# Value rows on ScalarE's queue, and the first rounding steps one stage later

## The chip, the cores and the metric

The kernel runs on one core of one Trainium2 chip. The metric is the device time of one execution in microseconds (us), lower is better. Where engines are named: TensorE (PE; PEld is its weight load), VectorE (DVE), ScalarE (ACT), GpSimd (POOL) and SyncE (SP, which only issues transfers).

## The reference

A retention layer (attention with a decay in place of the softmax) is followed by a feed-forward layer with the activation `h * erf(softplus(h))`. There are 8 batches, 8 heads, 576 tokens and 64 columns a head.

```python
scores = scale * np.matmul(q, k.transpose(0, 1, 3, 2))
Dmat = np.where(rel >= 0, gamma[:, None, None] ** rel[None, :, :], 0.0)
ret = scores * Dmat[None, :, :, :]
attn_out = np.matmul(ret, v)
# ... (B,H,S,D) -> (B*S, H*D) = x of 4608 x 512
h = x @ w_in                                  # w_in 512 x 2048
sp = np.maximum(h, 0.0) + np.log1p(np.exp(-np.abs(h)))
g = h * erf(sp)
out = g @ w_out                               # w_out 2048 x 512
```

## The kernel before

Attention is cut into 36 pieces of 128 tokens, counted from 0. Of each nine pieces the last is split: 64 tokens of each of two batches. Four pieces make a chunk of 512 tokens. A piece goes through three stages on TensorE: transposes of q and k, scores (masked by VectorE), and outputs, with a running state of k and v between the pieces of a batch.

```python
pieces = []
for b in range(0, B, 2):
    pieces += [[(b + j, s0, P, 0)] for j in range(2) for s0 in range(0, S - D, P)]
    pieces.append([(b + j, S - D, D, j * D) for j in range(2)])
...
SQUARES = 2 * PC        # from piece 8 on q comes in squares
SQUARES_K = 3 * PC      # from piece 12 on k comes in squares too
```

The "squares" are blocks laid out so that VectorE can transpose q and k in 32 x 32 blocks; earlier pieces are transposed by TensorE. Values `v` always come in rows, 256 bytes a packet, two transfers for a whole piece and four for a split one, into one of four buffers. Nearly all transfers are issued by SyncE, in the order in which they are written here:

```python
def load_squares(i, name, src):
    ...
            nc.sync.dma_start(out=t[...], in_=tokens[...])      # 4 for a piece, 8 for a split one

def load_rows(i, name, src, bufs):
    ...
    for b, s0, n, r0 in pieces[i]:
        for e in range(2):
            heads = src[b, e * NP : (e + 1) * NP, s0 : s0 + n, :]
            queue = nc.scalar if (name, i) == ("k", 0) else nc.sync
            queue.dma_start(out=t[r0 : r0 + n, e::2, :], in_=heads.rearrange("h p d -> p h d"))

def transposes(i):
    ...                                # q and k of the piece: kT, qT
    load(i + 2, "q")                   # squares of q, and of k from piece 12 on

def outputs(i):
    ...                                # o <- sT, v; o <- v, k; o <- qT, state; sums; x = scaled(1), scaled(0)
    load(i + 3, "kv")                  # rows of k and of v
    if i + 1 >= SQUARES:
        weigh_values(i + 1)            # GpSimd scales the rows of v by the decays

stages = [(transposes, 0), (scores, 0)]
for i in range(len(pieces)):
    stages += [(transposes, i + 1), (outputs, i), (scores, i + 1)]
```

Engines run their instructions in order. The buffers' semaphores and waits are set by the framework when the program is built.

The weights are rounded by VectorE, ScalarE and GpSimd before they are used. One part of the weights takes five steps, and between two steps the kernel may do other work:

```python
def rounding():
    while True:
        ...
        nc.scalar.activation(a_f, high_f, AF.Abs)
        nc.scalar.mul(out=r_f, in_=low, mul=2.0**-52)
        yield
        nc.vector.tensor_scalar(out=a_f, in0=a_f, ..., op0=ALU.max, op1=ALU.min)
        yield
        nc.vector.tensor_scalar(out=a, in0=a, ..., op0=ALU.logical_shift_left, op1=ALU.bitwise_and)
        yield
        nc.vector.scalar_tensor_tensor(out=a, in0=high, ..., op0=ALU.bitwise_and, op1=ALU.bitwise_or)
        yield
        ...                            # the rest: and, multiply, add
```

The order of the first stretch is written out in a string. `a` does the next attention stage, `l` loads rows of piece 2, `k` keeps TensorE warm with idle matmuls, `w` loads a part of the weights, a digit does so many rounding steps, `p` does a part of the first feed-forward product (`L565` in the profile), `s` stores x:

```python
for what in "alkakakawkakakawwaa3awa2aaa5ppppaa5wwppa5ppawappwcppa5ppaaapp5s":
    if what == "a":
        attend(done[0] + 1)
    ...
    else:
        round_weights(int(what))
```

Afterwards the attention stages are spread between the products of the feed-forward layer (`First`, `L511`, and `Second`, `L619`), each of which is evicted from PSUM by a copy of ScalarE or an addition of VectorE.

Of the kernel before, what the change touches and what calls it, by code (L numbers as in the profile page):

```python
# [54 lines left out]
def kernel(  # L55
# [10 lines left out]
    nc = tc.nc  # L66
# [53 lines left out]
    SQUARES_K = 3 * PC  # L120
# [15 lines left out]
    def load_rows(i, name, src, bufs):  # L136
        if name == "q":
            t = raw.tile([P, NP, P * D // SQ], FP32, tag="qs", name="raw_q", bufs=bufs)
            t = t.rearrange("p a x -> p (a x)")[:, : H * D].rearrange("p (h d) -> p h d", h=H)
        else:  # L140
            t = raw.tile([P, H, D], FP32, tag=name, name=f"raw_{name}", bufs=bufs)
        for b, s0, n, r0 in pieces[i]:
            for e in range(2):
                heads = src[b, e * NP : (e + 1) * NP, s0 : s0 + n, :]

                queue = nc.scalar if (name, i) == ("k", 0) else nc.sync
                queue.dma_start(out=t[r0 : r0 + n, e::2, :], in_=heads.rearrange("h p d -> p h d"))  # L147
        return t

    def load(i, names="qkv"):  # L150
        if i < len(pieces):
            t = loaded.setdefault(i, {})
            for name in names:
                src = {"q": q, "k": k, "v": v}[name]
                if name == "q" and i < SQUARES:
                    t["q"] = load_rows(i, "q", q, 2)
                elif name == "q":
                    t["qs"] = load_squares(i, "q", q)
                    if i >= SQUARES_K:
                        t["ks"] = load_squares(i, "k", k)  # L160
                elif name == "v" or i < SQUARES_K or len(pieces[i]) == 1:
                    t[name] = load_rows(i, name, src, 4)
# [69 lines left out]
    def load_weights():  # L232
        part = next(coming, None)
        if part is not None:
            t = wraw.tile([P, 2 * WP], UINT32, tag="wraw", name="wraw")
            for rows, src in part[0]:
                nc.sync.dma_start(out=t[rows].rearrange("p (h f) -> p h f", h=2), in_=src)
            words.append((t, *part[1:]))
# [49 lines left out]
    def round_weights(n=1):  # L288
        for _ in range(n):
            next(round_step, None)  # L290
# [174 lines left out]
    def attend(upto):  # L465
        while done[0] < min(upto, len(stages)):
            of, i = stages[done[0]]
            of(i)
            done[0] += 1
# [9 lines left out]
    def store_x(c):  # L479
        nc.sync.dma_start(out=xd[c], in_=x[0, c][:, :n_dc])  # L480
# [269 lines left out]
    def keep_busy(n):  # L750
        for _ in range(n):
            nc.tensor.matmul(idle[:, :P], lhsT=ones, rhs=ones, start=True, stop=True)
# [13 lines left out]

    for what in "alkakakawkakakawwaa3awa2aaa5ppppaa5wwppa5ppawappwcppa5ppaaapp5s":
        if what == "a":  # L770
            attend(done[0] + 1)
        elif what == "p":
            next(products)
        elif what == "s":
            store_x(0)
        elif what == "l":
            load(2, "kv")
        elif what == "c":
            nc.sync.dma_start(out=cst[:, CONST_FIRST:], in_=consts[:, CONST_FIRST:])
        elif what == "w":  # L780
            load_weights()
        elif what == "k":
            keep_busy(2)
        else:
            round_weights(int(what))
# [93 lines left out]
```

## Time and profile before

| what | value |
|---|---|
| time, median of 3 | 1020.92 us (1018.78 to 1022.29) |
| span of the profiled execution | 1019.8 us |
| TensorE clock granted | 1.000 |
| busy: TensorE / VectorE / ScalarE / GpSimd | 1008.4 / 662.0 / 390.0 / 120.0 us |
| moved by the transfers | 165.76 MB, mean 163 GB/s |
| packets under 512 bytes | 97376 of 146986 |

Busy time of an engine is the sum of its instructions; a matmul's end is modelled, so a full TensorE is not TensorE at its peak. The profile gives for each instruction what its engine waited for before it (the releaser). The attention pieces are loaded and computed in the first 318 us, with the feed-forward products of the first of four groups of weights running between them; after that only feed-forward work is left. A transfer shows as an issue on a queue (`SPq`, `ACTq`) and as a landing some microseconds later.

### The profile page before, as it was taken

To read this page: it belongs to the slowest core of one execution; us is meant where nothing else is said; L and a number is where in the kernel's file an instruction comes from. 1 tells how busy PE (TensorE), PEld (TensorE's weight loads), DVE (VectorE), ACT (ScalarE), POOL (GpSimd) and SP (SyncE) were. 2 spreads that over 40 slices of the span, in tenths; PEclk is the share of its full clock that TensorE was granted. 3 is DMA by queue.
4 is the path that set the end of the run, shared out by engine and by line. 5 is a ranking of instruction groups with operands and counts; after the bars stand their busy time and mean duration, and the time that the engine had idled before them with its cause. 6 is when DMAs were issued, how large, how long until landed. Compare 5 with 4: busy or idle time off the path is not lost.

```text
span 1019.8 us, 15964 instructions
## 1 busy us (share of the span) xinstructions
PE 1008.4 (99%) x6348; PEld 878.4 (86%) x6348; DVE 662.0 (65%) x1062; ACT 390.0 (38%) x481; POOL 120.0 (12%) x122
## 2 busy tenths in 40 slices
PE   8999999999999999999999999999999999999998
PEld 7788888887888888888888888888888888888887
DVE  3769867876976655666666666666667555555555
ACT  2354143233234443433343344434433333333332
POOL 2133121221212100010011001000100000000000
PEclk9999999999999999999999999999999999999999
DMA  9997989979976344544444344434333334444434
GB/s 195 205 245 171 237 193 220 241 159 248 245 160 240 115 158 147 162 159 146 166 146 145 130 165 159 145 145 145 145 124 124 135 124 131 125 131 139 124 88 119
DMA packets 146986, 165.76 MB, mean 163 GB/s; under 512 B 97376, under 2 KB 121568, under 8 KB 138848
## 3 DMA queue, kind: packets, MB, share of 16 engines
q1 hardware_dynamic: 144832, 163.57, 56.9%
q10 hardware_dynamic: 2080, 1.18, 0.5%
q8 instruction: 50, 0.82, 0.4%
q14 instruction: 24, 0.20, 0.1%
HBM read 117.52 MB, written 47.19 MB: 162 GB/s over the span
## 4 chain that ended last, share of the span: by engine, by line
PE 87%; DMA 6%; SPq 4%; DVE 2%; issue 0%; POOL 0%; ACT 0%; DVEq 0%; POOLq 0%; ACTq 0%
PE a L619 23%; PE a L511 22%; PE g L619 11%; PE g L511 11%; PE e L511 6%; PE e L619 6%; PE s L347 2%; PE o L365 2%; SPq L147 2%; SPq L131 2%; DMA raw_qs<-in_q_dram 1%; DMA raw_v<-in_v_dram 1%; DMA raw_ks<-in_k_dram 1%; DMA wraw<-in_moe_w_in_dram 1%; PE o L388 1%; PE o L377 1%
## 5 line engine op out<-in xcount | busy, mean ns | idle before, releaser
L511 PE MATMUL a<-x,wa 128*128 128x256 f32 x1088 | 257.3, 379 | 0.0
L511 PEld LDWEIGHTS a<-x,wa 128*128 128x128 f32 x1088 | 206.6, 190 | 28.2 <-issue 0.2
L619 PE MATMUL a<-wb,s 128*128 128x256 f32 x840 | 198.7, 380 | 0.0
L619 PEld LDWEIGHTS a<-wb,s 128*128 128x128 f32 x840 | 159.5, 190 | 22.0 <-ACT o L633 0.5
L99 DVE TENSOR_TENSOR t<-g,t 128x512 f32<-128x512 f32 x68 | 47.0, 690 | 148.3 <-ACT t L541 111.3
L511 PE MATMUL g<-x,wa 128*128 128x256 f32 x544 | 129.0, 380 | 0.0
L511 PEld LDWEIGHTS g<-x,wa 128*128 128x128 f32 x544 | 103.0, 190 | 14.3
L99 DVE TENSOR_TENSOR o<-a,o 128x512 f32<-128x512 f32 x104 | 71.5, 687 | 46.4 <-PE a L619 46.4
L536 ACT COPY t<-a 128x512 f32<-128x512 f32 x34 | 19.9, 585 | 177.7 <-PE a L511 177.7
L99 DVE TENSOR_TENSOR t<-t,s 128x1024 f32<-128x1024 f32 x72 | 85.0, 1222 | 0.0
L274 POOL TENSOR_TENSOR wraw<-wraw 128x512 f32<-128x512 f32 x28 | 29.4, 1051 | 446.0 <-DVE wraw L272 197.4
L580 ACT ACTIVATE s<-t 128x1024 f32<-128x1024 f32 x72 | 72.1, 1049 | 23.0 <-DVE t L99 23.0
L547 ACT COPY t<-a 128x512 f32<-128x512 f32 x34 | 19.9, 586 | 152.9 <-PE a L511 152.9
L99 DVE TENSOR_TENSOR x<-x 128x512 f32<-128x512 f32 x115 | 75.8, 693 | 1.2
L584 ACT ACTIVATE s<-s 128x1024 f32<-128x1024 f32 x72 | 72.1, 1048 | 0.4
L619 PE MATMUL g<-wb,s 128*128 128x256 f32 x280 | 66.8, 381 | 0.0
L619 PE MATMUL e<-wb,t 128*128 128x256 f32 x280 | 66.7, 381 | 0.0
L619 PE MATMUL g<-wb,t 128*128 128x256 f32 x280 | 66.2, 380 | 0.0
L619 PE MATMUL a<-wb,t 128*128 128x256 f32 x280 | 66.1, 379 | 0.0
L511 PE MATMUL e<-x,wa 128*128 128x256 f32 x272 | 64.9, 381 | 0.0
L541 ACT COPY t<-a 128x512 f32<-128x512 f32 x34 | 19.9, 585 | 108.7 <-PE a L511 108.7
L619 PEld LDWEIGHTS a<-wb,t 128*128 128x128 f32 x280 | 53.2, 190 | 7.2
(86 smaller groups left out, 1260.9 us busy)
## 6 DMA issues: line engine op xcount, KB each, us to landing
od<-o SPq DMA_DIRECT2D x54, 512.0 KB, 3.3
x<-xd SPq DMA_DIRECT2D x27, 1024.0 KB, 4.8
o<-od SPq DMA_DIRECT2D x27, 1024.0 KB, 5.0
raw_qs<-in_q_dram SPq DMA_DIRECT2D x96, 112.0 KB, 4.6
raw_ks<-in_k_dram SPq DMA_DIRECT2D x84, 112.0 KB, 4.1
xd<-x SPq DMA_DIRECT2D x9, 1024.0 KB, 5.5
raw_v<-in_v_dram SPq DMA_DIRECT2D x64, 128.0 KB, 4.4
wraw<-in_moe_w_in_dram SPq DMA_DIRECT2D x32, 256.0 KB, 5.8
```

Of the source, the lines that this page charges most:

```text
L99: nc.vector.tensor_tensor(out=out, in0=in0, in1=in1, op=op)
L131: nc.sync.dma_start(out=t[part * SQ : (part + 1) * SQ, :, at : at + m - SQ], in_=tokens[:, :, d0 : d0 + m - SQ])
L147: queue.dma_start(out=t[r0 : r0 + n, e::2, :], in_=heads.rearrange("h p d -> p h d"))
L274: engine.tensor_tensor(out=r_f, in0=high_f, in1=r_f, op=ALU.mult)
L347: nc.tensor.matmul(ps[e][:, p, :], lhsT=t["kT"][heads[e], p, :], rhs=t["qT"][heads[e], p, :], start=True, stop=True)
L365: nc.tensor.matmul(o[p % 2][heads[(e + p) % 2], p // 2, :], lhsT=t["v"][:, 2 * p + e, :], rhs=t["sT"][:, e, p, :], start=(p < 2), stop=(no ...
L511: nc.tensor.matmul(acc[:, j * TH : (j + 1) * TH], lhsT=weights["wa", self.g][:, a, d, j * P : (j + 1) * P], rhs=x[self.g, self.c][a][:, d, :],
L536: nc.scalar.copy(out=self.t1[:, 1], in_=self.a)
L541: nc.scalar.copy(out=self.t2[:, 1], in_=self.a)
L580: nc.scalar.activation(self.s[:, j], t, AF.Softplus)
L584: nc.scalar.activation(self.s[:, j], self.s[:, j], AF.Erf)
L619: nc.tensor.matmul(acc[:, tp, :], lhsT=left[:, j * TH + tp * P : j * TH + (tp + 1) * P], rhs=weights["wb", self.g][:, b, j, :], start=(sta ...
```

## The change

```diff
-                queue = nc.scalar if (name, i) == ("k", 0) else nc.sync
+
+                by_act = (name, i) == ("k", 0) or (name == "v" and i >= SQUARES_K)
+                queue = nc.scalar if by_act else nc.sync
                 queue.dma_start(out=t[r0 : r0 + n, e::2, :], in_=heads.rearrange("h p d -> p h d"))
...
-    for what in "alkakakawkakakawwaa3awa2aaa5ppppaa5wwppa5ppawappwcppa5ppaaapp5s":
+    for what in "alkakakawkakakawwaaa3wa2aaa5ppppaa5wwppa5ppawappwcppa5ppaaapp5s":
```

The first edit moves the rows of values of piece 12 and all later ones (the 13th piece on) from SyncE's queue to ScalarE's. SyncE has then fewer transfers to issue, and the squares of q and k stand behind fewer others in its queue; the values are issued where ScalarE stands in its own instructions. Nothing is added to what is moved.

The second edit exchanges one `3` and one `a` of the string: the first three steps of the first part's rounding (`3`) now come behind the outputs of the third piece (`a`) and not ahead of them, so that VectorE does the sums and the scaling of those outputs first. Both edits leave all arithmetic as it is.

## The prediction

> **What bounds the kernel now.** I read the page first: engine totals, then who waited for whom on TensorE, then busy time by stretches of 10 us.
>
> ```profile
> span 1019.8 us, 15964 instructions
> PE 1008.4 (99%) x6348; PEld 878.4 (86%) x6348; DVE 662.0 (65%) x1062; ACT 390.0 (38%) x481; POOL 120.0 (12%) x122
> PE s L347 <- DVE kT L326: 2.4, 1, 2.4
> PE pt_q L332 <- DVE x L99: 1.5, 1, 1.5
> PE pt_k L332 <- DMA raw_k<-in_k_dram: 1.0, 2, 0.6
> PE pt_q L332 <- DMA raw_q<-in_q_dram: 0.6, 1, 0.6
> 20.00:30.00 10.00, 8.47 (x139) 6.93 (x137) 6.65 (x15) 3.23 (x6) 2.16 (x3) 1.00 1.00 206
> 210.00:220.00 10.00, 10.00 (x97) 8.56 (x96) 8.04 (x15) 1.49 (x3) 1.61 (x2) 1.00 0.63 141
> 250.00:260.00 10.00, 7.59 (x81) 6.62 (x78) 7.96 (x15) 0.66 (x2) 2.10 (x3) 1.00 1.03 189
> ```
>
> In the rows of stretches the numbers after the length are the busy us of PE, PEld, DVE, ACT, POOL, then clock, DMA share, GB/s. TensorE is busy 99% of the span, and from 320 to 1000 us without a gap, so nothing can be won there by moving loads. All its idle time is 1019.8 - 1008.4 = 11.4 us; the four waits listed are 5.5 us of it. One wait of 1.5 us (25 us) is what the second edit aims at; one of 2.4 us (254 us) is a late piece of k, which the first edit might cure. That caps the gain at 3.9 us, 0.4%. The question is whether the change adds waits between 75 and 310 us, where attention pieces are loaded.
>
> **What the skill says.** "DMA: Bandwidth & Descriptors", section "Issuing engines are not separate DMA queues": transfers started by different engines run on the same 16 DMA engines, and a second issuer saves the sequencer's issue time alone. The trace agrees that this time is real: an issue of value rows takes SyncE 0.53 us (median of 80). The same page, section "Anatomy of one DMA", says that a wait for a semaphore is made by the issuing sequencer before dispatch. The trace agrees: SyncE stood 6.8 us in front of L131 for landings of value rows it had issued itself. So a queue behind an unmet wait stops with everything behind it, on ScalarE its compute too.
>
> **Part 1: the order of the first rounding.** PE's work is unchanged. On VectorE the list of instructions shows one move: the two clamps and shifts of the first weight part go behind `sums`, `x`, `x` of the third piece.
>
> ```profile
> 22.62 1.16 PE L347 MATMUL s<-qT,kT 64*128 64x128 f32 x16
> 23.64 0.43 DVE L259 TENSOR_SCALAR wa<-wa 128x512 f32<-128x512 f32 x1 [3.15 <-ACT wa L254]
> 24.44 0.42 DVE L99 TENSOR_TENSOR sums<-o,state 128x256 f32<-128x256 f32 x1
> 25.24 0.66 PE L332 MATMUL pt_q<-ident,raw_q 128*128 128x128 f32 x4 [1.46 <-DVE x L99]
> 34.31 0.63 PE L332 MATMUL pt_q<-ident,raw_q 128*128 128x128 f32 x4 [0.65 <-DMA raw_q<-in_q_dram]
> 35.29 0.66 PE L332 MATMUL pt_k<-ident,raw_k 128*128 128x128 f32 x4 [0.35 <-DMA raw_k<-in_k_dram]
> ```
>
> The outputs' matmuls end at 22.70, so `sums` can start at 22.73 instead of 24.44, and the first `x` frees its bank before TensorE ends the scores at 23.78: the 1.46 us wait goes. But VectorE still does the same five operations before the masking, 1.80 us from the first of them (23.64) to the masking (25.44), so masking starts at 22.73 + 1.80 = 24.53, not 25.44: 0.91 us earlier is what TensorE keeps. It then reaches the next transposes of q at 33.6 - 0.9 = 32.7, and those wait for transfers that landed at 34.17 (q) and 35.25 (k), issued at 26.6 to 29.8 behind four weight loads that no engine holds up. So most of the 0.9 us is waited away at 34 us. I count 0.5 us as an estimate, with 0 to 0.9 possible.
>
> **Part 2: value rows on ScalarE's queue.** SyncE loses 54 issues (21 whole pieces of 2, three split ones of 4; the built program has 692 transfers on SyncE before, 638 after), 54 x 0.53 = 28.6 us of issue time over 230 us. ScalarE gains the same 28.6 us. It is busy 110.6 of the first 320 us and mostly waits for TensorE, so that cost alone is hidden. Counting pieces from 0, piece 26 shows what isn't:
>
> ```profile
> 217.51 2.81 SPq L131 DMA_DIRECT2D raw_ks<-in_k_dram  x6
> 220.43 2.59 SPq L147 DMA_DIRECT2D raw_v<-in_v_dram  x4
> 222.02 0.45 DVE L326 STREAM_TRANSPOSE kT<-raw_ks 128x256 f32<-128x256 f32 x1 [1.47 <-DMA raw_ks<-in_k_dram]
> 223.13 0.58 ACT L536 COPY t<-a 128x512 f32<-128x512 f32 x1 [2.87 <-PE a L511]
> 225.11 1.16 PE L347 MATMUL s<-qT,kT 64*128 64x128 f32 x15
> ```
>
> Here SyncE issues squares of k at 217.5, they land by 222.0, VectorE transposes them by 222.47, and the scores run at 225.11 with 2.6 us to spare. In the built program every transfer counts on one of eight semaphores, handed out across both queues, and waits until the previous one on the same semaphore has landed. With one queue the previous one is always eight issues back. With two it is set in the built order, in which ScalarE's values stand early. There the seventh of the eight squares of k of piece 26 waits for the values of piece 28, which ScalarE issues only behind the copy that ends at 223.13 + 0.58 = 223.71. Then: landing of rows by ScalarE's queue 3.5 us (its two transfers of piece 0, part 6 of the page), 227.2; two issues of squares, 0.43 each, the second at 227.65; landing of a 48 KB square 2.0 us (part 6), 229.65; second transpose 0.45 us: 230.1. Scores at 230.1 instead of 225.11: **5.0 us** on the path, since TensorE is in order.
>
> The other pieces that gain such a wait, with 3.5 us for values, 0.43 us an issue, 3.0 us for a 112 KB square (an estimate between its shortest 1.8 and median 3.7 in the view by tile) and 1.09 us for kT:
> - Piece 19: values of 20 behind a copy ending 150.00; +3.5, three issues 1.3, +3.0, +1.09 = 158.9; scores at 158.92 before.
> - Piece 20: 158.12 + 3.5 + seven issues 3.0 + 3.0 + 1.09 = 168.7; before 169.20.
> - Piece 18: 139.72 + 3.5 + 3.0 + 3.0 + 1.09 = 150.3; before 150.96.
> - Piece 24: 195.20 + 3.5, two rows of k 1.0, eight squares 3.4, + 3.0 + 1.09 = 207.2; before 206.27: 0.9 late.
> - Piece 29: 245.53 + 0.5 + 3.5 + 3.0 + 1.09 = 253.6; before 253.95, so the 2.4 us wait stays.
>
> All but one of these end within 1 us of need; with median landings half would be late. I count 1.5 us for them together (the 0.9 and part of the others, as they overlap), and 0.5 us for VectorE, which stands still while kT waits and is 80% busy there.
>
> **Sum.** +5.0 (piece 26) +1.5 (other pieces) +0.5 (VectorE behind) -0.5 (rounding) = +6.5 us; 1020.9 + 6.5 = 1027.4, which I round to 1027.5 us.
>
> **The rivals.**
> 1. The purpose is met: SyncE runs earlier, squares land earlier, the 2.4 us wait at 254 us goes and 0.5 us at the start: 1020.9 - 2.9 = 1018 us. For it: at 210 to 230 us the DMA share is 0.63 while SyncE issues one small square after another, so SyncE's issue rate is the limit there and values in its way cost. Against it: the new waits above, at the very place.
> 2. The DMA engines are the bound and the order is all that changes: their share is 1.0 to 1.1 in 140 to 170 and 230 to 280 us. Values come 5 to 15 us early and push squares back by about their own 1.1 us a piece, which the spare 1.5 to 4 us of most pieces hide: 1020 to 1021 us.
> 3. The queues lock together: ScalarE waits for squares that SyncE is late with (the values of 18 wait for rows of k, those of 26 for stores of outputs), so its copies and erf come late, and SyncE waits for ScalarE again. Then each of some twenty pieces loses about 1 us: 1035 to 1045 us. Against it: by the landings of before, nearly all transfers that ScalarE would wait for landed well before it gets there.
>
> **Range and chances.** Rival 1 sets the low end, rival 3 most of the high end: 1018 to 1039 us. 2% is 20.4 us; faster by that is not in reach (all of TensorE's idle time is 11.4 us), slower needs rival 3 in full. Faster 0.01, within 0.92, slower 0.07.
>
> **What would show it.** In the profile after: the wait of `pt_q` for `x` at 25 us gone and that for q and k at 34 to 35 us longer; SyncE's waits in front of L131 naming `raw_v` with far more than 6.8 us; a wait of TensorE's scores for kT of about 5 us near 225 to 235 us; the 2.4 us wait at 254 still there; from 330 us on, the same work at the same pace. I am wrong if scores near 225 us don't wait (rival 1 or 2), or if waits of 1 us and more appear from 110 us on at most pieces, with ScalarE waiting for transfers (rival 3).

## The result and the profile after

The kernel after takes **1053.1 us** (median) against 1021.2 us of the kernel before beside it: ratio 1.031, 95% interval 1.028 to 1.033. It is slower by 3.1%, where the prediction had 1027.5 us and at most 1039. The profile below is of the fastest of its six runs (1048.0 us, mean granted clock 0.991; the others 1051.0 to 1054.9 at 0.985 to 0.989), so it holds 26.4 of the 31.9 us by which the medians differ.

The page of the kernel after, as far as it answers to the lines shown of before; in the second line the busy us of each engine, its share of the span and its instructions:

```profile
span 1046.2 us, 15974 instructions
PE 1017.2 (97%) x6348; PEld 882.9 (84%) x6348; DVE 662.6 (63%) x1062; ACT 390.0 (37%) x481; POOL 117.7 (11%) x122
PEclk9999999998999999999999999999999999999999
```

The span of the profiled run grew by 26.4 us in two parts. TensorE's idle time went from 11.4 to 29.0 us (+17.6), and its busy time from 1008.4 to 1017.2 us (+8.8) with the same 6348 matmuls. The digit 8 in the row of the clock points to the second part: before, that row held nines only.

Who waited for whom in the kernel after (us in total, times, longest); the last three lines are SyncE's queue from 95 to 345 us:

```profile
PE s L349 <- DVE kT L328: 19.2, 10, 5.1
PE pt_k L334 <- DMA raw_k<-in_k_dram: 1.8, 3, 0.6
PE g L513 <- DVE o L99: 1.3, 2, 0.7
...
SPq L131 <- DMA raw_v<-in_v_dram: 59.0, 22, 6.5
SPq L131 <- DMA raw_qs<-in_q_dram: 8.5, 9, 1.5
SPq L149 <- DMA raw_v<-in_v_dram: 6.5, 2, 4.6
```

(Lines of the program lie two further down than before: `L131` is unchanged, `L347` is now `L349`.) TensorE's wait of scores for kT was 2.4 us in all, once; now it is 19.2 us, ten times. One line points to the cause: SyncE stands 59 us in front of squares, waiting for values to land, 6.8 us before. It needs no values itself; in the built program it waits because of a semaphore that it shares with them. The wait of `pt_q` for `x` (1.5 us) is gone. These changes of waits (16.8 + 1.3 - 1.5, and +0.5 for rows of q and k at the start) make 17.1 of the 17.6 us of idle time.

Busy time by stretches (after the length: PE, PEld, DVE, ACT, POOL, then clock, DMA share, GB/s):

```profile
120.00:130.00 10.00, 7.29 (x78) 5.92 (x76) 5.72 (x10) 0.29 (x1) 0.43 (x1) 0.86 0.79 220
240.00:250.00 10.00, 4.24 (x36) 3.44 (x26) 5.15 (x9) 0.65 (x2) 0.86 (x2) 0.67 0.67 192
```

At 240 to 250 us TensorE works 4.24 of 10 us and the DMA engines are at 0.67: neither is the bound, the queues are standing. From 350 us on both kernels do the same work at the same pace, and the whole loss has been made by then (the last piece's outputs start at 343.1 us, 26.7 us later than the 316.4 of before).

Piece 26, the one of the prediction, in the list of instructions of the kernel after:

```profile
234.82 8.33 SPq L131 DMA_DIRECT2D raw_ks<-in_k_dram  x8
238.31 0.59 ACT L538 COPY t<-a 128x512 f32<-128x512 f32 x1 [2.87 <-PE a L513]
238.39 0.93 ACTq L149 DMA_DIRECT2D raw_v<-in_v_dram  x2
242.36 0.79 SPq L131 DMA_DIRECT2D raw_ks<-in_k_dram  x2
244.85 0.45 DVE L328 STREAM_TRANSPOSE kT<-raw_ks 128x256 f32<-128x256 f32 x1 [6.28 <-DMA raw_ks<-in_k_dram]
245.44 2.08 PE L349 MATMUL s<-qT,kT 64*128 64x128 f32 x16 [5.08 <-DVE kT L328]
```

Eight issues that take 3.4 us in a row take 8.33: the seventh goes off at 242.36, as the values of piece 28, which ScalarE issues at 238.39 beside its copy, land. The two last squares, their landing, the transpose and the scores follow. TensorE had been free since 240.36 (245.44 less the 5.08 of idle time before it).

### The profile page after: what moved, and what is told of

It reads as the page before. It is cut to its first block, busy times and chain, and to the rows that moved or that the text cites. A ratio compares the mean times of both kernels' runs of the same rounds, so it can differ in the third digit from the quotient of the medians.

```text
span 1046.2 us, 15974 instructions
## 1 busy us (share of the span) xinstructions
PE 1017.2 (97%) x6348; PEld 882.9 (84%) x6348; DVE 662.6 (63%) x1062; ACT 390.0 (37%) x481; POOL 117.7 (11%) x122
## 4 chain that ended last, share of the span: by engine, by line
PE 81%; DMA 9%; DVE 4%; SPq 3%; ACT 2%; issue 1%; ACTq 0%; POOL 0%; DVEq 0%
PE a L621 22%; PE a L513 21%; PE g L513 11%; PE g L621 11%; PE e L621 5%; PE e L513 5%; DMA raw_v<-in_v_dram 4%; DMA raw_ks<-in_k_dram 2%; SPq L131 2%; PE s L349 2%; PE o L367 1%; SPq L149 1%; DVE t L99 1%; DMA raw_k<-in_k_dram 1%; DVE kT L328 1%
## 5 line engine op out<-in xcount | busy, mean ns | idle before, releaser
L513 PE MATMUL a<-x,wa 128*128 128x256 f32 x1088 | 259.9, 382 | 0.0
L513 PEld LDWEIGHTS g<-x,wa 128*128 128x128 f32 x544 | 104.2, 192 | 16.8 <-DVE o L99 2.4
L349 PE MATMUL s<-qT,kT 64*128 64x128 f32 x576 | 42.7, 288 | 19.6 <-DVE kT L328 19.2
```

What stands on the lines that cost most here:

```text
L349: nc.tensor.matmul(ps[e][:, p, :], lhsT=t["kT"][heads[e], p, :], rhs=t["qT"][heads[e], p, :], start=True, stop=True)
L513: nc.tensor.matmul(acc[:, j * TH : (j + 1) * TH], lhsT=weights["wa", self.g][:, a, d, j * P : (j + 1) * P], rhs=x[self.g, self.c][a][:, d, :],
```

## The experiments

Two theories stood at the start. **Theory:** the two queues count on the same eight semaphores, so SyncE's squares wait for values that ScalarE issues late. **Rival:** the values' bytes come at another time, and the 16 DMA engines bring the squares late, whatever the semaphores. Smaller questions were which of the two edits counts, and where the 8.8 us of slower matmuls come from.

### One edit at a time

The order of rounding alone, values on SyncE (against the kernel before):

```diff
-    for what in "alkakakawkakakawwaa3awa2aaa5ppppaa5wwppa5ppawappwcppa5ppaaapp5s":
+    for what in "alkakakawkakakawwaaa3wa2aaa5ppppaa5wwppa5ppawappwcppa5ppaaapp5s":
```

> The order of the first rounding alone, all values back on SyncE. Theory (this edit gains what the start of the trace after shows): the scores of piece 5 at 38.7 us instead of 39.3, the wait of pt_q for x at 25 us gone, and from there the same as before: 1020.5 us, 0.6 below before, ratio 0.9994. Rival (given back at the waits of 245 to 255 us, or by another hand-out of the semaphores): the same as before or up to 1 us slower. Neither expects more than 2 us either way.

Measured: 1022.8 us, ratio 1.0001 (0.9991 to 1.0011). The wait for `x` goes, and the scores of piece 5 start at 38.95 us instead of 39.29. At 255 us kT is waited for 2.35 us as before, and two waits of 0.33 and 0.51 us come at 244 to 247 us that before had not, so nothing of the early gain is left in this trace. The interval is 1 us wide to each side: a gain of the 0.5 us that was predicted is neither shown nor excluded.

The values alone, with the old order of rounding (against the kernel after):

```diff
-    for what in "alkakakawkakakawwaaa3wa2aaa5ppppaa5wwppa5ppawappwcppa5ppaaapp5s":
+    for what in "alkakakawkakakawwaa3awa2aaa5ppppaa5wwppa5ppawappwcppa5ppaaapp5s":
```

> The values on ScalarE's queue alone, the order of rounding as before. Theory (the whole loss is of this edit): 1053.5 us, ratio 1.03, waits of the scores for kT of 15 to 22 us in some ten pieces from 115 us on, SyncE's waits in front of the squares for values above 50 us. Rival (the two edits act on each other, the 0.6 us of the start shifts ScalarE against SyncE): under 1045 us.

Measured: 1052.3 us, ratio 1.029 (1.027 to 1.032); kT waits 20.7 us in seven stands, SyncE 62.7 us in front of squares for values. The loss is of this edit: its interval and that of the kernel after (1.028 to 1.033) largely overlap.

### The same values, on semaphores of their own

Both edits, with the values issued by GpSimd (against the kernel after):

```diff
-                queue = nc.scalar if by_act else nc.sync
+                queue = nc.scalar if i == 0 and name == "k" else nc.gpsimd if by_act else nc.sync
```

> Both edits, but the values of piece 12 on go by GpSimd's queue, at the same place in the program; in the built program these transfers count on semaphores of their own, so no transfer of SyncE waits for values, and values reach the chip about as late as from ScalarE. Theory (the loss is SyncE standing before squares for semaphores it shares with values): no wait of SyncE for raw_v after piece 16, waits of the scores for kT under 4 us in sum, 1019 to 1023 us. Rival A (values at another time in the 16 DMA engines' work push the squares late, whatever the semaphores): 1035 us and more, kT waits of 10 us and more. Rival B (GpSimd's issues cost it so much time that weighing the values comes late): waits of the outputs for raw_v instead, 1025 us and more.

Measured: **1019.2 us**, ratio 0.9974 (0.9962 to 0.9986), faster than both kernels. The page, and the row of these transfers (count, KB, median us to landing):

```profile
span 1017.1 us, 15969 instructions
PE 1009.1 (99%) x6348; PEld 877.6 (86%) x6348; DVE 666.4 (66%) x1062; ACT 390.5 (38%) x481; POOL 162.8 (16%) x176
raw_v<-in_v_dram POOLq DMA_DIRECT2D x42, 128.0 KB, 6.9
```

No scores wait for kT at all; the 2.4 us wait of before at 254 us is gone too. The values still leave early (those of piece 28 at 226.6 us; SyncE issued them at 240.7 before) and land more slowly than on ScalarE's queue (6.9 us against 4.3): moving the bytes early does not hurt the squares, so the rival falls. Rival B as well: GpSimd is 45 us busier than in the kernel after, and one wait of 0.3 us for its weighing is all that TensorE sees. Even here SyncE stands some 44 us in front of `L131` for transfers, all of its own queue (14.1 us of it for rows of k), and no scores wait for it. So the length of SyncE's stands is not the cost; it matters what it stands for.

Without the new order of rounding (against the version just shown):

```diff
-    for what in "alkakakawkakakawwaaa3wa2aaa5ppppaa5wwppa5ppawappwcppa5ppaaapp5s":
+    for what in "alkakakawkakakawwaa3awa2aaa5ppppaa5wwppa5ppawappwcppa5ppaaapp5s":
```

> Values on GpSimd's queue with the old order of the first rounding. Theory (the new order's 0.6 us at the start is kept where no wait for squares follows): 1019.7 us, 0.5 above the version with both, the wait of pt_q for x of 1.5 us back at 25 us. Rival (the order is worth nothing in any case, as alone it measured 1.0001): 1019.2 us.

Measured: 1019.3 us, ratio 0.9983 (0.9973 to 0.9992). No difference from the version with both that the intervals could tell apart; the wait for `x` was 0.6 us, where 1.5 was expected.

### Only the semaphores, without the bytes

Values stay on GpSimd's queue (this edit is against that version with both edits); at each of their places ScalarE issues 32 bytes that nobody reads. The row written is scratch; no part of the computation changes.

```diff
                 queue.dma_start(out=t[r0 : r0 + n, e::2, :], in_=heads.rearrange("h p d -> p h d"))
+                if queue is nc.gpsimd:
+                    tiny = raw.tile([1, H], FP32, tag="tiny", name="tiny", bufs=4)
+                    nc.scalar.dma_start(out=tiny, in_=consts[0:1, :H])
```

> As the version with values on GpSimd's queue (which lost nothing), but at each of those places ScalarE issues a transfer of 32 bytes from the constants into a scratch row that nobody reads. These share SyncE's eight semaphores in the way the values did; in the built program 94 transfers of SyncE wait for one of them. No bytes to speak of, and nobody needs them. Theory (the loss is SyncE's and ScalarE's queues holding each other through the shared semaphores): kT waits of 10 us and more return, with SyncE's waits for tiny, 1035 to 1055 us. Rival (the loss is the time at which ScalarE's 7 MB of values move, or GpSimd's queue helps in another way): 1019 to 1022 us.

Measured: 1045.8 us, ratio 1.024 (1.021 to 1.027). Its waits, the second line again of SyncE's queue from 95 to 345 us:

```profile
PE s L352 <- DVE kT L331: 17.7, 6, 6.3
...
SPq L131 <- DMA tiny<-in_decays_dram: 56.5, 19, 5.9
```

54 transfers of 32 bytes bring back about 27 us on the version that had no loss (ratio 1.024 against 0.9974), four fifths of the 34 us between that version and the kernel after. SyncE stands 56.5 us for bytes that nobody needs. (47 transfers of SyncE wait for one of them in the built program; the 94 of the expectation is twice too many.) This shows the cause with next to nothing added to what the DMA engines have to move.

The control: SyncE issues the 32 bytes.

```diff
-                    nc.scalar.dma_start(out=tiny, in_=consts[0:1, :H])
+                    nc.sync.dma_start(out=tiny, in_=consts[0:1, :H])
```

> A control for the run with transfers of 32 bytes: the same 54 transfers at the same places of the program, values again on GpSimd's queue, but SyncE issues the 32 bytes instead of ScalarE. They count on the same eight semaphores; none of SyncE's transfers then waits for one that another engine has yet to issue. Theory (the loss comes of two engines sharing the semaphores): 1019 to 1023 us, kT waits under 3 us. Rival (54 more transfers on eight semaphores cost it, whoever issues them): 1030 us and more.

Measured: 1021.7 us, ratio 1.0006 (0.9989 to 1.0024), kT waits 1.4 us. The same transfers on the same semaphores cost about 3 us on the version without them (1.0006 against 0.9974) when SyncE issues them, and 27 us when ScalarE does.

### Values one piece earlier

A fifth buffer for values; the idle matmuls' tile of ones is halved to make room.

```diff
-                    t[name] = load_rows(i, name, src, 4)
+                    t[name] = load_rows(i, name, src, 5 if name == "v" else 4)
...
-        load(i + 3, "kv")
+        load(i + 3, "k")
+        if i + 3 < SQUARES_K:
+            load(i + 3, "v")
+        if i + 4 >= SQUARES_K:
+            load(i + 4, "v")
...
```

> Both edits, values on ScalarE's queue, but each is issued one piece earlier in the program (fifth buffer for values), so ScalarE reaches it some 8 to 10 us earlier; the semaphores stay shared. Theory (SyncE waits because ScalarE reaches the values late): most of the loss goes, waits of the scores for kT under 6 us, 1020 to 1030 us. Rival (ScalarE's reach doesn't matter, it stands itself before values for semaphores of SyncE's squares, and the two queues hold each other all the same): 1040 us and more, with ScalarE's waits for raw_qs and raw_ks above 20 us.

Measured: 1056.5 us, ratio 1.034 (1.032 to 1.036). SyncE's queue from 95 to 345 us, and TensorE's scores:

```profile
PE s L349 <- DVE kT L328: 20.5, 8, 5.2
...
SPq L131 <- DMA raw_v<-in_v_dram: 60.7, 23, 5.4
```

The form of the theory that this run tested, that the loss goes when ScalarE reaches the values sooner, is wrong. The built program says why: in the kernel after, 34 of the 43 waits of SyncE for values are squares of piece p for values of piece p+1; in this one 28 of 47 are squares of p for values of p+2. The semaphores are handed out in the built order; with values a piece earlier, they were shared with squares a piece earlier. That the distance in time therefore stayed is inferred from these counts and from SyncE's 60.7 us against 59.0; it was not measured. The rival's sign came true by its letter: the profile puts 29.4 us of ScalarE's idle time down to squares, where it expected over 20. But these are four idle times (5.6 to 11.4 us), and each of the copies behind them starts within 0.04 us of the end of the product that it reads, so TensorE released it (shown below for the kernel after).

### Fewer pieces

```diff
-                by_act = (name, i) == ("k", 0) or (name == "v" and i >= SQUARES_K)
+                by_act = (name, i) == ("k", 0) or (name == "v" and i >= 24)
```

> Both edits, but values go by ScalarE's queue only from piece 24 on, so 12 pieces instead of 24. Theory (every piece whose squares share a semaphore with late values can stall, wherever the change begins): no wait of the scores for kT over 1 us before 200 us, two to four of 1 to 5 us after it, about half the loss: 1030 to 1040 us. Rival A (the stalls feed on each other, and without those of 126 to 188 us the later ones stay hidden, as the prediction's sum from the kernel before has it): 1022 to 1028 us, with at most one stall of 5 us. Rival B (full loss from any use): 1045 us and more.

Measured: 1039.1 us, ratio 1.017 (1.015 to 1.019). Half of the pieces, a little over half of the loss. No kT wait over 0.3 us before 216 us, then five of 1.2 to 5.8 us (13.8 us in all); piece 26 has the longest again:

```profile
232.55 2.08 PE L349 MATMUL s<-qT,kT 64*128 64x128 f32 x16 [5.81 <-DVE kT L328]
```

So stalls need no earlier stalls, and the prediction's picture of one bad piece does not hold even for a change that begins right before that piece: TensorE stands 1.2 to 3.5 us before pieces 25, 29, 32 and 33 as well.

### The slower matmuls

The kernel before, with a gap put in at piece 26:

```diff
         t = live[i]
+        if i == 26:
+            for _ in range(11):
+                nc.scalar.copy(out=t["kT"], in_=t["kT"])
```

> The kernel before with one wait put in: ahead of the scores of piece 26 (225 us) ScalarE copies kT onto itself eleven times, so that TensorE stands some 4 to 5 us there; no transfer changes. Theory (a stand of TensorE's lowers its granted clock for the next 8 us, and a gap of 5 us costs 2 to 4 us more than itself): granted clock under 0.85 in the 10 us after the gap, matmuls of 128x256 of 0.42 us instead of 0.21 there, 1028 to 1031 us. Rival (the slower clock of the kernel after came from something else in it): 1.00 after the gap, 1026 to 1027 us.

Measured: 1027.0 us, ratio 1.0055 (1.0038 to 1.0073). The gap was longer than meant:

```profile
230.93 2.08 PE L350 MATMUL s<-qT,kT 64*128 64x128 f32 x16 [6.35 <-ACT kT L345]
232.94 3.58 PE L514 MATMUL g<-x,wa 128*128 128x256 f32 x8
236.35 1.89 PE L514 MATMUL a<-x,wa 128*128 128x256 f32 x8
...
220.00:230.00 10.00, 4.58 (x60) 3.71 (x58) 5.33 (x9) 6.54 (x11) 1.61 (x2) 0.97 0.64 147
230.00:240.00 10.00, 9.07 (x42) 7.50 (x44) 4.33 (x7) 2.55 (x5) 3.33 (x3) 0.69 1.10 270
```

Scores take 2.08 instead of 1.16 us behind the gap and the first eight matmuls of g 3.58 instead of 1.99, at a clock of 0.69 in that stretch: 2.5 us beside the gap's own 6.35. (The later wait of 2.4 us at 254 us went, as the squares had more time, and that for `x` was 1.0 us shorter: 6.35 + 2.5 - 2.4 - 1.0 = 5.5. The span grew by 5.5 us, and the ratio says 5.6.)

The gap filled with matmuls whose result nobody reads, behind the eleven copies, first 44 of them:

```diff
+            fill = [ps_at.tile([P, NP, P], FP32, tag="at", name=f"fill{e}") for e in range(2)]
+            for n in range(44):
+                nc.tensor.matmul(fill[n % 2][:, 0, :], lhsT=ident, rhs=ident, start=True, stop=True)
```

> The same wait at the same place, but TensorE spends it on 44 matmuls of 128x128 whose result nobody reads (about 4.7 us at 0.107 us each). Theory (it is the standing still that lowers the clock): 1.00 throughout, 1026 to 1028 us, 2 to 3 us under the kernel with the bare gap. Rival (the delay of the work itself, or the late copies of ScalarE behind, make the later work slow): the same time as with the bare gap.

Measured: 1029.4 us, ratio 1.0075 (1.0046 to 1.0104). As a comparison of times it failed: the filling took 10.1 us instead of 4.7, longer than the gap. The clock was 1.00 throughout.

Then with `range(27)`:

> The filled gap again with 27 matmuls instead of 44: the 44 took 10.1 us (each stands as two records of 0.115 us), longer than the gap of 6.35 us that they were to fill; 27 should take 6.2 us. Theory (standing still lowers the clock): 1.00 throughout, the scores behind the gap in 1.2 us instead of 2.1, 1024.5 us, 2.5 under the kernel with the bare gap. Rival (the late work makes the later work slow): 1027 us as with the bare gap.

Measured: 1025.1 us, ratio 1.0032 (1.0019 to 1.0045).

```profile
226.04 6.29 PE L348 MATMUL fill<-ident 128*128 128x128 f32 x54
233.13 1.16 PE L353 MATMUL s<-qT,kT 64*128 64x128 f32 x16 [0.79 <-ACT kT L345]
234.22 1.99 PE L517 MATMUL g<-x,wa 128*128 128x256 f32 x8
...
230.00:240.00 10.00, 9.21 (x69) 7.99 (x70) 5.03 (x9) 4.96 (x9) 4.76 (x5) 1.00 1.07 271
```

The scores come 7.1 us behind the outputs, 6.35 in the bare gap, but they and the matmuls behind them run at full speed. Less the 6.29 us of filling TensorE is busy for 1008.6 us, where it was 1011.1 with the bare gap and 1008.4 before: this is the 2.5 us. The ratio is 0.23% lower, 2.3 us, but the two intervals overlap a little, and the spans of the two profiled runs are the same (1025.2 and 1025.3 us; the filled one had more waits elsewhere), so the time only agrees and it is the trace that shows it. Standing still lowers the clock, and this costs on top of the stand.

## Why the prediction was wrong, point by point

**What held.** TensorE was the bound and little could be won: the version with values on GpSimd's queue won 2.7 us by its ratio (1.4 to 3.9), where the prediction had 3.9 as the cap. SyncE's wait in front of `L131` for `raw_v` grew as said, and the mechanism, a shared semaphore, is the one that the experiments show. For **piece 26** the sum came out, with everything 15 us later: values issued beside the copy, landed 4.0 us after (3.5 predicted), two issues 0.79 us (0.86), landing of the last square 2.1 us from its issue at 242.7 (2.0), transpose 0.45 us; TensorE stood 5.08 us, 5.0 predicted. The closeness is partly luck: ScalarE issued the values 0.5 us before its copy ended, where the sum began, and they landed 0.5 us later than the sum had it.

**What failed: the term "+1.5 (other pieces)".** It measured 14.1 us of stands (19.2 less the 5.1 of piece 26) in nine pieces, 11.7 us more than the 2.4 of before. Of these, 4.7 us fell on three pieces of the prediction's list (19, 24 and 29) and 9.4 us on six that it did not have (15, 21, 23, 25, 32 and 33). The prediction itself wrote that with median landings half of its list would be late, and still counted 1.5 us. Three things were wrong in it.

1. *Landing of values, 3.5 us.* I took it from ScalarE's two transfers at the start. The view by line, first of the kernel before for those two, gives us from issue to landing:

```profile
L147 ACTq DMA_DIRECT2D raw_k<-in_k_dram x2: 512/527/542, 0.7 to 1.3; - x2
DMA to landing us min/median/max: 3.2/3.5/3.9
```

and of the kernel after, for the values that piece 19 waits for, and then for all of ScalarE's from 95 to 345 us:

```profile
L149 ACTq DMA_DIRECT2D raw_v<-in_v_dram x2: 374/446/519, 153.4 to 153.8; - x2
DMA to landing us min/median/max: 6.8/7.1/7.3
...
L149 ACTq DMA_DIRECT2D raw_v<-in_v_dram x50: 374/520/2252, 96.2 to 316.7; - x50
DMA to landing us min/median/max: 2.3/4.2/7.3
```

For piece 19 the prediction had 3.5 + 1.3 + 3.0 + 1.09 = 8.9 us from the end of the copy to kT, against 8.9 at hand, and called it free. Landing alone took 3.3 to 3.8 us more (6.8 and 7.3), and TensorE stood 2.93 us. The median of 4.2 us would not have been enough either; where a chain has less than 1 us to spare, the longest landings decide, and the page of before had the median of value rows at 4.4 us.

2. *"0.43 us an issue."* Piece 15 was not in my list. By the list's own figures, with eight issues for 3.4 us, it was free: 111.8 + 3.5 + 3.4 + 3.0 + 1.09 = 122.8, before its scores at 124.0. In the kernel after:

```profile
111.81 1.71 ACTq L149 DMA_DIRECT2D raw_v<-in_v_dram  x2
116.37 1.76 SPq L131 DMA_DIRECT2D raw_qs<-in_q_dram  x4
118.23 4.03 SPq L131 DMA_DIRECT2D raw_ks<-in_k_dram  x4
124.95 1.08 DVE L328 STREAM_TRANSPOSE kT<-raw_ks 128x512 f32<-128x512 f32 x1 [2.19 <-DMA raw_ks<-in_k_dram]
126.19 1.16 PE L349 MATMUL s<-qT,kT 64*128 64x128 f32 x16 [2.71 <-DVE kT L328]
```

The four squares of k took 4.03 us, 1.81 before. Where ScalarE's values take places in the round of eight, SyncE's own transfers meet again after four, and the third and fourth square of k waited for squares of q issued just before to land. That is the line of 8.5 us for `raw_qs` among SyncE's waits, which before had none in front of `L131`.

3. *The third rival was dismissed by the landings of before.* "Nearly all transfers that ScalarE would wait for landed well before it gets there" was true, and was the wrong question. ScalarE is hardly held up. The profile names squares of q or rows of k for four of its long idle times (6.2 to 10.7 us), but each copy there starts within 0.05 us of the end of the product that it reads. (A late load of weights did hold it once: a rounding step at 195.81 us after 11.66 us, and the copy behind it 3.0 us late; the values at 197.51 left on time.) One of the four:

```profile
127.28 3.67 PE L513 MATMUL a<-x,wa 128*128 128x256 f32 x8
130.98 0.59 ACT L549 COPY t<-a 128x512 f32<-128x512 f32 x1 [10.69 <-DMA raw_qs<-in_q_dram]
```

(127.28 + 3.67 = 130.95.) What replaces the picture of two queues that hold each other is a leash. ScalarE follows TensorE; values follow ScalarE; squares follow values through the semaphore; TensorE needs the squares a piece later. From the copy at 111.75 to the scores of piece 15 that took 14.4 us, with 11.7 us of work for TensorE in it; for piece 19 13.2 us with 10.2. Before, SyncE ran ahead as far as buffers let it, and most pieces had 2 to 5 us between kT and scores. So the outcome I gave the third rival, about 1 us for each of some twenty pieces, was near, by another way: 19.2 us of stands on 24 pieces. With the clock on top of it even its 1045 us was too low, and the 2% that the prediction gave to that rival alone were passed without it.

**What was missing: the clock.** No term of the sum had these 8.8 us. Five groups behind the stands of pieces 15, 21 and 26 are 7.0 of the 8.8 us: eight matmuls of `a` at 127 us in 3.67 instead of 1.89, eight of `e` at 189 us in 3.64 instead of 1.99, and behind piece 26 scores 2.08 for 1.16, `g` 3.78 for 1.99, `a` 2.79 for 1.89. The rest was not traced.

**Small terms.** Rounding, -0.5: too small to be measured. VectorE behind, +0.5: 1.3 us (`g` waiting for `o`). Of the 2.4 us wait at 254 us I said that it stays; piece 29 stands 1.3 us in the kernel after. In all, the trace has +5.1 (piece 26) +11.7 (other pieces) +1.3 (VectorE) -1.5 (`x`) +0.5 (rows of q and k) +8.8 (clock) and 0.5 of small waits: the 26.4 us of the span.

What stays open: why in the kernel after just these ten pieces stand and others with the same kind of wait don't was followed for pieces 15, 19 and 26 only. Values on ScalarE's queue with semaphores of their own were not tried.

## What to carry to other kernels

Before you move transfers to a second queue, ask what they count on: if two in-order queues share semaphores, the one that ran ahead is tied to the slower engine's program, and here even 32 bytes were enough. Look for a queue that counts by itself and whose engine has idle time. And when several waits with little to spare are added, size each by the longest landings in that stretch rather than by one from a quiet stretch, and add the cost of a stand of TensorE to the stand itself.

## What the runs showed of the hardware that was not expected

A stand of TensorE was followed by matmuls at half speed: 0.43 us instead of 0.22 us for one of 128x256, at a granted clock of 0.50 for some 5 us after the gap of 6.35 us and 8 us after that of 5.08. The Trainium skill has it, "TensorE: Matmul & The Clock Gate", section "What's actually happening": the clock is halved after an idle window of about 3.4 us and given back after a busy one, and the window runs freely, whatever the program does. The halving and the free-running window agree; but a window need not be idle throughout. Stands of 2.71 us (piece 15) and 1.84 us (piece 21) halved the clock, one of 2.93 us (piece 19) did not. In the kernel after the changes of the clock between 100 and 300 us (127.29, 130.70, 188.73, 192.14, 243.34 and 253.58 us) lie on one grid of 3.41 us. Busy times in windows of this grid, around pieces 15, 19 and 21, columns as above:

```profile
123.87:127.29 3.42, 1.10 (x17) 1.01 (x17) 2.30 (x4) 0.00 (x0) 0.00 (x0) 1.00 0.88 249
127.29:130.70 3.41, 3.41 (x10) 2.78 (x9) 3.41 (x8) 0.00 (x0) 1.13 (x2) 0.50 0.93 269
161.42:164.83 3.41, 2.08 (x35) 1.61 (x33) 0.71 (x1) 0.59 (x1) 0.00 (x0) 1.00 0.99 321
164.83:168.25 3.42, 1.81 (x19) 1.67 (x20) 3.02 (x5) 0.00 (x0) 0.00 (x0) 1.00 1.12 268
168.25:171.66 3.41, 3.41 (x17) 3.00 (x17) 3.41 (x8) 0.38 (x1) 0.00 (x0) 1.00 0.61 163
185.31:188.73 3.42, 1.58 (x29) 1.24 (x22) 2.47 (x4) 0.00 (x0) 0.00 (x0) 1.00 0.92 207
188.73:192.14 3.41, 3.41 (x9) 2.70 (x10) 3.41 (x8) 0.00 (x0) 1.38 (x2) 0.50 1.13 217
```

The longer stand of piece 19 was split by the boundary at 164.83 us: TensorE was idle for 39% and 47% of two windows. Those of pieces 15 and 21 left one window idle for 68% and 54%, and the next had half the clock. Read in this way, the traces of all thirteen kernels hold 18 windows at full clock with 61% of idle time or more, and half the clock followed each; it followed none with up to 48%, and one of the four between 53% and 56%. So what a stand costs here depends on where it falls, and one of 1.84 us was enough.

Issues from GpSimd cost it about 0.8 us each (45 us for 54, on an engine whose spans are rough), and their rows landed in 6.9 us (median) against 4.3 us by ScalarE's queue. Both were hidden here.
